# Attention beside a two-layer MLP on one core: one attention slot between any two parts of layer 1, a new order of each engine's work within a slot, and a second batch with float32 second products

## The chip, the cores and the metric

The kernel runs on one core of one Trainium2 chip. The metric is the device time of one execution in microseconds (us). A core has five engines that each take their own instructions strictly in order and wait for one another through semaphores: TensorE (PE; its weight loads are shown apart as PEld), VectorE (DVE), ScalarE (ACT), GpSimd (POOL), and SyncE (SP), which here only issues transfers. Matrix products land in PSUM, eight banks of 128 x 512 float32; everything else lives in SBUF.

## What is computed

Four batches, eight heads, 576 positions, head size 64. Attention is masked by blocks of 64, its output is the input of two dense layers with a nonlinearity between their halves; all arithmetic keeps float32 precision.

```python
scores = scale * np.matmul(q, k.transpose(0, 1, 3, 2))       # 4 x 8 heads, 576 x 576
scores = np.where(block_i >= block_j, scores, -1000000000.0)  # blocks of 64
scores = scores - np.max(scores, axis=-1, keepdims=True)
attn = np.exp(scores)
attn = attn / (np.sum(attn, axis=-1, keepdims=True) + 1e-09)
x = np.matmul(attn, v)                                        # -> 2304 tokens x 512
h = x @ w_in                                                  # layer 1: 512 -> 2048 -> 512
x = (np.maximum(h, 0.0) + alpha * np.minimum(h, 0.0)) @ w_out
h = x @ w2_in                                                 # layer 2, same sizes
out = np.where(h > 0.0, h, np.exp(np.minimum(h, 0.0)) - 1.0) @ w2_out
```

## The kernel before, in words

**Split products.** Most products are made of two-part numbers: a value is rounded to float32r ("high") and the rest is kept as a second float32r number ("low", made by `low_part`). A layer's product then takes three passes (high x high, high x low, low x high). The products of the layers are groups of 12 matmuls of 128 x 512.

**Attention.** Heads are taken in 16 pairs, four pairs to a batch. A pair is cut into five slots, and `slot(k)` handles slot `i = k % 5` of pair `k // 5`: its scores on PE (into one of two PSUM tiles, `pair0` and `pair1`, in turn), the row maxima on DVE, the exponentials on ACT, then the normalising factors on DVE and the normalising itself on POOL (`p`). The same call also transposes on PE what was exponentiated four slots earlier (`LAG = 4`) and moves the result out of PSUM into the tile `pt`.

**Second products** (attention weights times v). For the first `WHOLE` pairs `pt` is moved once, as float32, and the second products are float32, with the two heads of a pair in the two column halves of the array (`emit_pv_whole`). For the other pairs `pt` and v are split into a high and a low part (ACT and DVE for `pt`, POOL for v), and the products are float32r (`emit_pv`): head x = 0, then x = 1, each followed by an ACT copy and a DVE addition into the tile `xt`, from which POOL makes the two parts of x. Each pair has two halves: queries 0 to 255 ("half 0") and 256 to 575 ("half 1").

**Beside it.** When batch u is done, layer 1's first half of hidden units is run on it while the attention of batch u + 1 goes on (`l1_beside`): 8 "h parts" (12 matmuls, an ACT copy `h`, an ACT `neg`, a DVE `g`, an ACT and a POOL operation for the two parts of `g`), then 8 "y parts" of 12 matmuls. `att_events` gives every slot and every second product a cost, and the loop at the end of the kernel runs events until their cost has kept up with the parts done. PSUM bank 7 holds layer 1's products, banks 4 to 6 take transposes and second products in turn.

**Weights.** `load_w` fetches a 128 x 1024 block of weights and rounds it in five stages, each issued a given number of ticks after the load (`later`): ACT reads it (`wword`), DVE cuts the bits, POOL adds, ACT rounds (`w`, high), DVE subtracts (`w`, low). There are two buffers for the raw block and two for `wword`. Six blocks are loaded in the lead (before layer 1 starts), ten beside batch 1, and 48 in the rest.

**The rest.** After the attention follow steps of one h group and, two steps later, one y group: layer 1's first half on the last two units ("A"), its second half on all five ("B"), layer 2 ("C"). Units are 512, 512, 512, 512 and 256 tokens. Weights are loaded at the steps that `w_at` names.

Of the kernel before, what the change touches and what calls it, by code (L numbers as in the profile page):

```python
# [19 lines left out]
P = 128  # L20
# [21 lines left out]
def attention_moe_kernel(ctx: ExitStack, tc: tile.TileContext, qT, kT, v_a, v_b, w1, w2, alpha, out):  # L42
# [134 lines left out]
    WHOLE = 4  # L177
# [108 lines left out]
    def transposes(n, i):  # L286
# [66 lines left out]
    def emit_pv_whole(n, half):  # L353
# [11 lines left out]
        parts, tail = parts_of_x(n, half)  # L365
        for c, dst in parts:
            act.copy(dst(0), op[:, c])
            low_part("v", dst(1), op[:, c], dst(0))
        x_out(n, half, tail)

    def emit_pv(n, half):
# [3 lines left out]
        xt = ap1.tile([P, 320], F32, tag="xt", name="xt")  # L375
        op = None
        for x in range(2):
            if half or not x:
                op = bank[take("o")]
            o_ = op[:, qn * x:qn * x + qn] if half == 0 else op[:, :qn]  # L380
            for j in range(nch):
                rows = 64 if j == 4 else P
                lo, o = max(0, P * j - q0), place(half, j)
                for k in range(2):
                    pe.matmul(o_[:, lo:qn], s["vs"][:rows, 5 * x + j, :, :].rearrange("p a d -> p (a d)"),  # L385
                              s["pt", half, k][:rows, x, o + lo:o + qn],
                              start=j == 0 and k == 0, stop=j == nch - 1 and k == 1, skip_group_check=True)
            main, other = slice(64 * x, 64 * x + 64), slice(64 - 64 * x, 128 - 64 * x)
            act.copy(xt[main, :qn], o_[other, :])
            dve.tensor_tensor(out=xt[main, :qn], in0=o_[main, :], in1=xt[main, :qn], op=ALU.add)  # L390
        parts, tail = parts_of_x(n, half)
        for c, dst in parts:
            copy("p", dst(0), xt[:, c])
            low_part("p", dst(1), xt[:, c], dst(0))
        x_out(n, half, tail)
# [3 lines left out]
    COST_S, COST_T = (.33, .35, .5, .7, .8), (.22, .44, .66, .88, .5)  # L399
    LAG = 4  # L400
    NS = 5 * len(PAIRS)

    def slot(k):
# [7 lines left out]
        if i == 0 and n:  # L411
            normalise(n - 1, 2)
        if here:
            maxima(n, i)
        if move:
            move()
        if here:
            exponentials(n, i)
            if i == 0 and n + 1 < len(PAIRS):
                load_pair(n + 1)  # L420
            if i == 1:
                load_v(n)

    def att_events():
        slots = {}

        def at(k, order, cost, emit, done=None):
            here = slots.setdefault(k, [])
            here.append((order, len(here), cost, emit, done))

        for k in range(NS + LAG):
            cost = (COST_S[k % 5] if k < NS else 0) + (COST_T[(k - LAG) % 5] if k >= LAG else 0)
            at(k, 0, cost, lambda k=k: slot(k))
        for n, (b, p) in enumerate(PAIRS):
            k = 5 * n
            if n + 1 < len(PAIRS):
                at(k + 2, 3, 0, lambda n=n: split_k(n + 1))
                at(k + 3, 3, 0, lambda n=n: split_q(n + 1))
            last = b if p == NPAIR - 1 else None
            pv = emit_pv_whole if n < WHOLE else emit_pv  # L440
# [262 lines left out]
```

## Time and profile before

| | us |
|---|---|
| median of three runs | 1184.72 (1184.21 to 1184.79) |
| the profiled execution, its own time | 1185.07 |
| its span from the first to the last instruction | 1183.0 |
| PE busy | 1032.0 (87%) |
| DVE busy | 607.7 (51%) |
| ACT busy | 473.6 (40%) |
| POOL busy | 399.4 (34%) |

How to read it: busy time is an average over stages that are limited by different things. The first scores start at 5.6 us. The lead (attention alone) ends at 93.9 us, when layer 1's first group starts; the first groups of the units beside batches 1, 2 and 3 start at 93.9, 243.4 and 360.0 us; the attention is over and stage A begins at 468.7 us; B's first group starts at 548.0 and C's at 759.8 us. The profile names an instruction by its line, the engine, the tile written and the tiles read, with the shapes. An idle time is put down to the instruction that ended it.

### The profile page before, as it was taken

The page shows a single profiled execution, that of the slowest core. Times are in us where ns is not written, and L with a number is a line of the kernel's source. Part 1 is how long each engine was busy: PE and PEld are TensorE (multiplying, and loading weights), DVE is VectorE, ACT ScalarE, POOL GpSimd, SP SyncE. Part 2 cuts the span into 40 slices and gives each one's busy share as a digit, 9 for nine tenths or more (in the row PEclk, how much of TensorE's full clock was granted, in tenths as well). Part 3 has the DMA queues.
Part 4 walks back from the last instruction along what each step waited for, and adds up shares of the span by engine and source line. Part 5 has one row for each costly group of instructions (what it writes and reads, how often), then busy time and mean ns, then how long its engine had stood idle before and what let it go on. Part 6 is the DMA issues. An engine that isn't in the chain of part 4 may idle for free.

```text
span 1183.0 us, 14068 instructions
## 1 busy us (share of the span) xinstructions
PE 1032.0 (87%) x5072; PEld 839.8 (71%) x5072; DVE 607.7 (51%) x1087; ACT 473.6 (40%) x1037; POOL 399.4 (34%) x484
## 2 busy tenths in 40 slices
PE   6867657888888798987899999969899999999998
PEld 4545445666666677876788888857688888888887
DVE  5765777445544552655354564576753333333343
ACT  4655554335534551545333434444432222222222
POOL 5655656445644642544344344422200000000000
PEclk9878787988899989988899999989999999999999
DMA  3432321112121012354355444442120020010000
GB/s 98 146 102 97 105 90 51 68 51 68 51 88 48 30 40 95 115 194 139 130 168 171 160 134 169 161 179 89 54 107 1 1 107 1 1 71 1 1 37 18
DMA packets 50468, 101.57 MB, mean 86 GB/s; under 512 B 10592, under 2 KB 18784, under 8 KB 49760
## 3 DMA queue, kind: packets, MB, share of 16 engines
q1 hardware_dynamic: 50400, 100.69, 25.1%
q8 instruction: 40, 0.66, 0.2%
q14 instruction: 28, 0.23, 0.1%
HBM read 72.36 MB, written 28.31 MB: 85 GB/s over the span
## 4 chain that ended last, share of the span: by engine, by line
PE 53%; DVE 20%; ACT 13%; issue 6%; DMA 4%; POOL 4%; SPq 1%; ACTq 0%; POOLq 0%; DVEq 0%
PE bank L544 14%; PE bank L526 13%; PE bank L480 7%; PE bank L503 6%; PE bank L568 5%; DMA wraw<-w 3%; DVE wword L132 3%; PE bank L385 3%; DVE w L81 3%; DVE g L467 2%; ACT wword L125 2%; ACT wraw L126 2%; DVE wword L131 2%; PE pair L234 2%; ACT p L264 2%
## 5 line engine op out<-in xcount | busy, mean ns | idle before, releaser
L480 PE MATMUL bank<-x,w 128*128 128x512 f32 (+1 forms) x960 | 223.8, 385 | 4.3 <-DVE z L87 2.4
L544 PE MATMUL bank<-w,gs 128*128 128x512 f32 x864 | 213.9, 394 | 15.5 <-DVE z L575 9.1
L526 PE MATMUL bank<-x,w 128*128 128x512 f32 (+1 forms) x960 | 210.2, 368 | 0.0
L480 PEld LDWEIGHTS bank<-x,w 128*128 128x128 f32 x960 | 175.7, 199 | 37.3 <-DVE z L87 3.6
L544 PEld LDWEIGHTS bank<-w,gs 128*128 128x128 f32 x864 | 162.1, 190 | 52.3 <-issue 9.5
L526 PEld LDWEIGHTS bank<-x,w 128*128 128x128 f32 x960 | 169.1, 188 | 31.1
L81 POOL TENSOR_TENSOR gs<-g,gs 128x512 fp32r<-128x512 f32 (+1 forms) x80 | 96.5, 1206 | 224.5 <-ACT gs L470 212.9
L568 PE MATMUL bank<-gs,w 128*128 128x512 f32 (+1 forms) x672 | 149.8, 371 | 19.1 <-ACT z L85 8.8
L568 PEld LDWEIGHTS bank<-gs,w 128*128 128x128 f32 x672 | 118.5, 197 | 42.7 <-ACT z L85 9.4
L137 POOL TENSOR_TENSOR wword<-wword,wraw 128x512 int32<-128x512 int32 x64 | 92.7, 1449 | 93.7 <-DVE wword L132 63.1
L531 DVE TENSOR_SCALAR e<-e 128x512 f32<-128x512 f32 (+1 forms) x80 | 32.0, 400 | 179.2 <-ACT e L530 179.2
L530 ACT ACTIVATE e<-bank 128x512 f32<-128x512 f32 (+1 forms) x80 | 44.1, 551 | 161.3 <-PE bank L526 161.3
L385 PE MATMUL bank<-pt,vs 128*128 128x320 f32 (+4 forms) x336 | 58.5, 313 | 47.1 <-DVE xt L390 45.3
L467 DVE SCALAR_TENSOR_TENSOR g<-neg,beta,bank 128x512 f32<-128x512 f32 (+1 forms) x56 | 37.5, 669 | 120.4 <-ACT neg L466 118.9
L88 POOL TENSOR_SCALAR p<-p,stat 128x128 f32<-128x128 f32 (+2 forms) x144 | 80.1, 573 | 40.4 <-DVE stat L275 23.1
L385 PEld LDWEIGHTS bank<-pt,vs 128*128 128x128 f32 (+1 forms) x336 | 53.1, 203 | 53.5 <-DVE xt L390 47.0
L125 ACT ACTIVATE wword<-wraw 128x512 f32<-128x512 f32 x64 | 42.9, 670 | 111.5 <-DVE w L81 74.6
L264 ACT ACTIVATE p<-pair,stat 128x128 f32<-128x128 f32 (+3 forms) x128 | 66.4, 526 | 42.0 <-DVE stat L253 35.8
L535 ACT CAST gs<-e 128x512 fp32r<-128x512 f32 (+1 forms) x80 | 46.2, 578 | 84.9 <-DVE e L532 84.9
L132 DVE SCALAR_TENSOR_TENSOR wword<-wraw,wword 128x512 uint32<-128x512 uint32 x64 | 78.4, 1225 | 2.2
L503 PE MATMUL bank<-gs,w 128*128 128x512 f32 x288 | 77.1, 422 | 2.2 <-ACT z L85 2.2
L81 DVE TENSOR_TENSOR gs<-e,gs 128x512 fp32r<-128x512 f32 (+1 forms) x80 | 51.0, 638 | 42.5 <-ACT gs L535 42.5
(84 smaller groups left out, 1278.3 us busy)
## 6 DMA issues: line engine op xcount, KB each, us to landing
wraw<-w SPq DMA_DIRECT2D x64, 512.0 KB, 3.7
xd<-x SPq DMA_DIRECT2D x16, 512.0 KB, 3.1
x<-xd SPq DMA_DIRECT2D x16, 512.0 KB, 8.6
yd<-ys SPq DMA_DIRECT2D x16, 512.0 KB, 3.4
x<-yd SPq DMA_DIRECT2D x4, 2048.0 KB, 8.3
qraw<-qT SPq DMA_DIRECT2D x16, 288.0 KB, 2.8
kraw<-kT SPq DMA_DIRECT2D x16, 288.0 KB, 3.2
vraw<-v_a SPq DMA_DIRECT2D x16, 256.0 KB, 3.3
```

What stands on the lines that cost most here:

```text
L81: return {"v": dve, "p": pool_e}[eng].tensor_tensor(out=out, in0=x, in1=f32(high), op=ALU.subtract)
L88: return pool_e.tensor_scalar(out, x, 1.0 if scale is None else scale, 1.0, ALU.mult, ALU.mult)
L125: act.activation(out=w, in_=high.bitcast(F32), func=AF.Abs)
L132: dve.scalar_tensor_tensor(out=wi, in0=high, scalar=0xC0000000, in1=wi, op0=ALU.bitwise_and, op1=ALU.bitwise_or)
L137: pool_e.tensor_tensor(out=w, in0=w, in1=units, op=ALU.add)
L264: act.activation(out=p[:, x, :], in_=sb[:, x, :ext], func=AF.Exp, bias=stat[:, o + x:o + x + 1], accum_out=stat[:, 4 + o + x:5 + o + x])
L385: pe.matmul(o_[:, lo:qn], s["vs"][:rows, 5 * x + j, :, :].rearrange("p a d -> p (a d)"), s["pt", half, k][:rows, x, o + lo:o + qn], start= ...
L480: pe.matmul(h, w_in(0, f, wp_, kc), x[:, xp_, kc, :n], start=kc == 0 and t == 0, stop=kc == KC - 1 and t == 2)
L503: pe.matmul(acc, w_out(0, f, wp_, m * P, P), gs[f][:, gp_, :n], start=f == 0 and t == 0, stop=f == FH - 1 and t == 2)
L526: pe.matmul(h, w_in(1, f, wp_, kc), x[:, xp_, kc, :], start=kc == 0 and t == 0, stop=kc == KC - 1 and t == 2)
L544: pe.matmul(acc, gs[:, gp_, tg * P:(tg + 1) * P], w_out(1, f, wp_, 0, DM), start=f == 0 and t == 0, stop=f == NF - 1 and t == 2)
L568: pe.matmul(acc, w_out(0, f, wp_, m * P, P), gs[:, gp_, :n], start=first and t == 0, stop=last and t == 2)
```

## The change

Five things change.

1. **A slot between any two parts.** Layer 1 beside a batch is cut into 20 parts (8 h parts of 12 matmuls, and 12 y parts of 9, 9 and 6), and one attention slot follows each. The list of events with costs is gone. The lead takes 27 slots (0 to 26) where it took 26.
2. **Second products inside a slot.** They are issued to PE right behind the slot's scores and ahead of its transposes; what empties their PSUM bank is issued behind the maxima and ahead of the moves of `pt`. Half 0 comes one slot later than before. Of a split pair, both heads of half 0 are issued before either is read, and the two heads of half 1 stand in two slots.
3. **The gate is held.** DVE's `g` of an h part is issued in the slot behind it, behind that slot's maxima, and its two parts behind the slot's exponentials.
4. **`WHOLE = 8`.** Batch 1 (pairs 4 to 7) has float32 second products as batch 0 has. Which of ACT and DVE moves which part of a float32 `pt` changes as well.
5. **Weights.** Eight blocks are loaded in the lead, one every third slot, and eight beside batch 1, one for each of its first eight parts. In stage A the last eight blocks of layer 1's second half are spread thinner (steps 8, 10, 12, 14 and 16 to 19); layer 2's first half is loaded at steps 20 to 35, one a step, where it was every other step from 19 to 49; its second half starts two steps before C, where it was four.

```diff
-    WHOLE = 4
+    WHOLE = 8
...
-                    copy("av"[(m + i) % 2], dst(pt[0]), src)
+                    copy("a" if m == 0 and i else "v", dst(pt[0]), src)
...
+    def products(k):
+        todo = []
+        n, i = divmod(k - LAG - 4, 5)
+        if i == 0 and 0 <= n < len(PAIRS):
+            todo += [lambda: pv_whole(n, 0)] if n < WHOLE else [lambda: pv(n, 0, 0), lambda: pv(n, 0, 1)]
+        m, i = divmod(k - LAG - 6, 5)
+        if 0 <= m < len(PAIRS) and i < 2:
+            if m >= WHOLE:
+                todo.append(lambda: pv(m, 1, i))
+            elif i == 0:
+                todo.append(lambda: pv_whole(m, 1))
+        return todo
...
         if here:
             scores(n, i)
+        outs = [p() for p in products(k)]
         move = transposes(*divmod(k - LAG, 5)) if 0 <= k - LAG < NS else None
...
         if here:
             maxima(n, i)
+        after = [h() for h in held]
+        held.clear()
+        for o in outs:
+            o()
         if move:
             move()
         if here:
             exponentials(n, i)
+        for a in after:
+            a()
...
-        pv = emit_pv_whole if n < WHOLE else emit_pv
-            at(k + LAG + 3, 2, .75, lambda n=n, pv=pv: pv(n, 0))
-            at(k + LAG + 6, 2, 2.3, lambda n=n, pv=pv: pv(n, 1), last)
...
-                if f % 4 == 3:
+                if f in (2, 5, 7):
...
-        W_AT = (8, 12, 16, 20, 24, 28)
+        lead = X_DONE[0] + 2
+        for k in range(lead):
+            if k % 3 == 0 and k and len(todo_w) > FH:
+                load_w(*todo_w.pop(0))
+            slot(k)
...
         for u in range(B - 1):
+            parts = l1_beside(u)
+            for j in range(20):
+                if todo_w:
+                    load_w(*todo_w.pop(0))
+                next(parts)
+                if k < LAST:
+                    slot(k)
+                    k += 1
...
+        spread = [*range(8), *range(8, 16, 2), *range(16, 20)]
-            w_at[i] = (0, FH + half[0], half[1])
-            w_at[first_of["B", 0] + lag + 1 + 2 * i] = (1, *half)
-            w_at[first_of["B", NU - 1] + lag + 2 + i] = (1, FH + half[0], half[1])
+            w_at[spread[i]] = (0, FH + half[0], half[1])
+            w_at[spread[-1] + 1 + i] = (1, *half)
+            w_at[first_of["C", 0] - 2 + i] = (1, FH + half[0], half[1])
```

PE's instructions around half 0 of a split pair, before: transposes (`ident`), the eight second products (`vs`) into bank 102, then layer 1's y part (`gs`) into bank 104.

```order
L310 MATMUL bank_103<-ident,p 128x128 x4
L310 MATMUL bank_101<-ident,p 128x128 x4
L385 MATMUL bank_102<-pt_1691,vs 128x256
L385 MATMUL bank_102<-pt_1692,vs 128x256
L385 MATMUL bank_102<-pt_1691,vs 128x128
L385 MATMUL bank_102<-pt_1692,vs 128x128
L385 MATMUL bank_102<-pt_1691,vs 128x256
L385 MATMUL bank_102<-pt_1692,vs 128x256
L385 MATMUL bank_102<-pt_1691,vs 128x128
L385 MATMUL bank_102<-pt_1692,vs 128x128
L503 MATMUL bank_104<-gs,w 128x512 x12
```

The same place in the changed kernel: an h part of layer 1 (`x`), the next slot's scores (`pair`), the eight second products, then the transposes.

```order
L499 MATMUL bank_104<-x_1061,w 128x512 x12
L234 MATMUL pair_100<-kh,qh 128x512 x2
L234 MATMUL pair_100<-kl,qh 128x512 x2
L234 MATMUL pair_100<-kh,ql 128x512 x2
L386 MATMUL bank_103<-pt_2068,vs 128x256
L386 MATMUL bank_103<-pt_2069,vs 128x256
L386 MATMUL bank_103<-pt_2068,vs 128x128
L386 MATMUL bank_103<-pt_2069,vs 128x128
L386 MATMUL bank_103<-pt_2068,vs 128x256
L386 MATMUL bank_103<-pt_2069,vs 128x256
L386 MATMUL bank_103<-pt_2068,vs 128x128
L386 MATMUL bank_103<-pt_2069,vs 128x128
```

The eight rows themselves are the same; what stands between the first four and the last four on the other engines has moved, as DVE's order shows. Before, DVE took `g` as soon as its h part was issued, and the two additions into `xt` behind it, ahead of the next slot's maximum (`stat<-pair`):

```order
L81 TENSOR_TENSOR pt_2323<-bank_101,pt_2322 128x4x128
L81 TENSOR_TENSOR pt_2323<-bank_102,pt_2322 128x4x128
L467 SCALAR_TENSOR_TENSOR g<-neg,beta,h 128x512
L390 TENSOR_TENSOR xt<-bank_103,xt 64x256 x2
L252 MEMSET pair_100 64x2x64
L253 TENSOR_REDUCE stat<-pair_100 128x2
```

Now the maximum comes first, then the held `g`, then the additions into `xt`, then the moves of `pt`:

```order
L252 MEMSET pair_99 64x2x64
L253 TENSOR_REDUCE stat<-pair_99 128x2
L482 SCALAR_TENSOR_TENSOR g<-neg,beta,h 128x512
L396 TENSOR_TENSOR xt<-bank_103,xt 64x256 x2
L81 TENSOR_TENSOR pt_2907<-bank_101,pt_2906 128x4x2x64
L81 TENSOR_TENSOR pt_2907<-bank_102,pt_2906 64x2x64
L211 SCALAR_TENSOR_TENSOR ql<-qraw,qh 128x512
```

So `g` and the additions moved behind the maximum of the slot that follows the h part.

ACT's instructions in a slot of the lead that has half 1 of a float32 pair, before: the move of `pt`, the exponentials (`p,stat<-pair`) of two slots with two weight operations between them, and then the two casts of x that empty the second products' bank.

```order
L85 COPY pt_521<-bank_101 128x2x128
L268 ACTIVATE p,stat<-pair_99,stat 128x576
L125 ACTIVATE wword<-wraw 128x512
L126 ACTIVATE wraw<-wraw 128x512
L264 ACTIVATE p,stat<-pair_100,stat 128x128 x2
L367 CAST x_312<-bank_104 128x256
L367 CAST xtail<-bank_104 128x64
```

Now the casts come first, then the move, then the slot's own exponentials:

```order
L268 ACTIVATE p,stat<-pair_99,stat 128x576
L370 CAST x_343<-bank_104 128x256
L370 CAST xtail<-bank_104 128x64
L85 COPY pt_536<-bank_102 128x2x256
L264 ACTIVATE p,stat<-pair_100,stat 128x128 x2
```

The exponentials moved behind the second products, the casts that read them, and the move.

## Rows read from the trace of the kernel before

**Rows 1.** Busy time by stage; the stretch and its length come first.

```profile
core 0: us, PE busy (x) PEld busy (x) DVE busy (x) ACT busy (x) POOL busy (x), PEclk, DMA share, GB/s
0.00:93.90 93.90, 64.83 (x375) 41.80 (x375) 61.49 (x151) 50.45 (x144) 53.67 (x91) 0.84 0.35 113
93.90:197.70 103.80, 62.80 (x308) 49.36 (x308) 75.86 (x123) 55.66 (x128) 61.40 (x70) 0.79 0.26 88
197.70:243.40 45.70, 40.53 (x219) 32.67 (x217) 20.76 (x49) 16.80 (x48) 21.48 (x37) 0.96 0.23 76
243.40:360.00 116.60, 97.30 (x524) 78.21 (x524) 58.65 (x130) 55.74 (x146) 63.08 (x96) 0.91 0.18 60
360.00:468.70 108.70, 92.37 (x483) 74.59 (x483) 49.00 (x105) 49.08 (x122) 51.74 (x77) 0.92 0.14 46
468.70:571.00 102.30, 87.23 (x433) 74.99 (x434) 59.31 (x87) 46.85 (x90) 46.74 (x35) 0.90 0.46 154
731.00:866.00 135.00, 116.88 (x579) 96.53 (x578) 90.84 (x139) 57.71 (x110) 38.83 (x31) 0.96 0.36 127
```

**Rows 2.** Who waited for whom, 93.9 to 468.7 us: total, times, longest.

```profile
PE bank L385 <- DVE xt L390: 45.3, 12, 7.9
...
DVE g L467 <- ACT neg L466: 45.7, 19, 4.7
...
PE bank L310 <- DVE pt L81: 12.3, 7, 3.6
```

**Rows 3.** Timeline, 253 to 258 us: start, length, instruction, idle before and its end.

```profile
253.48 0.57 PE L385 MATMUL bank<-pt,vs 128*128 128x256 f32 x4
...
255.15 0.75 DVE L467 SCALAR_TENSOR_TENSOR g<-neg,beta,h 128x512 f32<-128x512 f32 x1 [1.30 <-ACT neg L466]
...
256.58 0.37 ACT L389 COPY xt<-bank 64x256 f32<-64x256 f32 x1
...
256.98 0.42 DVE L390 TENSOR_TENSOR xt<-bank,xt 64x256 f32<-64x256 f32 x1 [1.08 <-ACT xt L389]
...
257.45 1.11 PE L385 MATMUL bank<-pt,vs 128*128 128x256 f32 x4 [3.40 <-DVE xt L390]
```

**Rows 4.** Timeline of PE in stage B, two groups that follow each other.

```profile
576.35 2.88 PE L480 MATMUL bank<-x,w 128*128 128x512 f32 x12
579.07 2.88 PE L568 MATMUL bank<-gs,w 128*128 128x512 f32 x12
```

**Rows 5.** Busy time of `wword` instructions alone: DVE, ACT, POOL, then clock and DMA.

```profile
0.00:93.90 93.90, 14.21 (x24) 7.72 (x12) 7.70 (x6) 0.84 0.35 113
93.90:197.70 103.80, 38.36 (x41) 12.86 (x20) 14.17 (x10) 0.79 0.26 88
```

**Rows 6.** Timeline of PE, half 0 of a float32 pair in the lead.

```profile
24.17 0.92 PE L362 MATMUL bank<-pt,vraw 128*64 128x256 f32 x8
```

**Rows 7.** Busy time by stretch, columns as rows 1: half 1 whole, then half 1 split.

```profile
30.87:34.90 4.03, 4.03 (x21) 1.85 (x20) 3.46 (x8) 1.76 (x7) 4.03 (x6) 0.58 0.66 240
266.88:270.10 3.22, 3.22 (x24) 2.94 (x21) 2.00 (x6) 2.37 (x7) 1.70 (x3) 1.00 0.18 69
```

**Rows 8.** Timeline of ACT in stage C, one weight block a step.

```profile
811.70 0.67 ACT L125 ACTIVATE wword<-wraw 128x512 f32<-128x512 f32 x1 [3.26 <-DVE w L81]
812.27 0.65 ACT L126 ACTIVATE wraw<-wraw 128x512 int32<-128x512 uint32 x1
...
818.50 0.67 ACT L125 ACTIVATE wword<-wraw 128x512 f32<-128x512 f32 x1 [3.26 <-DVE w L81]
```

**Rows 9.** Timeline, waits in stages A to C: a transfer and two PSUM banks.

```profile
533.93 0.66 ACT L125 ACTIVATE wword<-wraw 128x512 f32<-128x512 f32 x1 [8.69 <-DMA wraw<-w]
...
565.94 5.10 PE L568 MATMUL bank<-gs,w 128*128 128x512 f32 x12 [5.84 <-ACT z L85]
...
780.81 5.16 PE L544 MATMUL bank<-w,gs 128*128 128x512 f32 x12 [9.06 <-DVE z L575]
```

**Rows 10.** Who waited for whom in the lead, 0 to 93.9 us.

```profile
PE pair L234 <- ACT p L264: 8.7, 4, 3.7
```

More of the change, by code (lines that the diff above doesn't have):

```diff
@@ L364, in emit_pv_whole, with out, pv @@
                           start=j == 0, stop=j == nch - 1, skip_group_check=True)
[L365 to L371, printed above, removed]
+        def out():
+            parts, tail = parts_of_x(n, half)
+            for c, dst in parts:
+                act.copy(dst(0), op[:, c])
+                low_part("v", dst(1), op[:, c], dst(0))
+            x_out(n, half, tail)
+        return out
+    def pv(n, half, x):
         s = st[n]
@@ L374, in emit_pv @@
         nch = 2 if half == 0 else 5
[L375 to L387, printed above, removed]
-            main, other = slice(64 * x, 64 * x + 64), slice(64 - 64 * x, 128 - 64 * x)
-            act.copy(xt[main, :qn], o_[other, :])
-            dve.tensor_tensor(out=xt[main, :qn], in0=o_[main, :], in1=xt[main, :qn], op=ALU.add)
@@ L391, in emit_pv @@
[L391 to L399, printed above, removed]
+        if half or not x:
+            s["op"] = bank[take("o")]
+        op = s["op"][:, :qn] if half else s["op"][:, qn * x:qn * x + qn]
+        for j in range(nch):
+            rows = 64 if j == 4 else P
+            lo, o = max(0, P * j - q0), place(half, j)
+            for k in range(2):
+                pe.matmul(op[:, lo:], s["vs"][:rows, 5 * x + j, :, :].rearrange("p a d -> p (a d)"),
+                          s["pt", half, k][:rows, x, o + lo:o + qn],
+                          start=j == 0 and k == 0, stop=j == nch - 1 and k == 1, skip_group_check=True)
@@ new lines, in out @@
+        def out():
+            main, other = slice(64 * x, 64 * x + 64), slice(64 - 64 * x, 128 - 64 * x)
+            if x == 0:
+                s["xt"] = ap1.tile([P, 320], F32, tag="xt", name="xt")
+            xt = s["xt"]
+            act.copy(xt[main, :qn], op[other, :])
+            dve.tensor_tensor(out=xt[main, :qn], in0=op[main, :], in1=xt[main, :qn], op=ALU.add)
+            if x == 1:
+                parts, tail = parts_of_x(n, half)
+                for c, dst in parts:
+                    copy("p", dst(0), xt[:, c])
+                    low_part("p", dst(1), xt[:, c], dst(0))
+                x_out(n, half, tail)
@@ L403, in slot @@
+    held = []
     def slot(k):
@@ L418, in slot @@
             exponentials(n, i)
[L419 to L439, printed above, removed]
-            pv = emit_pv_whole if n < WHOLE else emit_pv
-            at(k + LAG + 3, 2, .75, lambda n=n, pv=pv: pv(n, 0))
-            at(k + LAG + 6, 2, 2.3, lambda n=n, pv=pv: pv(n, 1), last)
-            if n >= WHOLE:
-                at(k + LAG + 1, 3, 0, lambda n=n: split_v(n))
-        return [e[2:] for k in sorted(slots) for e in sorted(slots[k], key=lambda e: e[:2])]
-    def run(event):
-        cost, emit, _ = event
-        emit()
-        if cost:
-            end_tick()
+        for a in after:
+            a()
+        if i == 0 and n + 1 < len(PAIRS):
+            load_pair(n + 1)
+        if i == 1 and here:
+            load_v(n)
+        if i == 2 and n + 1 < len(PAIRS):
+            split_k(n + 1)
+        if i == 3 and n + 1 < len(PAIRS):
+            split_q(n + 1)
+        m, j = divmod(k - LAG - 2, 5)
+        if j == 0 and WHOLE <= m < len(PAIRS):
+            split_v(m)
+        end_tick()
+    X_DONE = [5 * (NPAIR * b + NPAIR - 1) + LAG + 6 + (NPAIR * (b + 1) > WHOLE) for b in range(B)]
     def load_x1(u):
@@ L466, in l1_gate, with gate @@
         act.activation(out=neg, in_=h, func=AF.Relu, scale=-1.0)
-        dve.scalar_tensor_tensor(out=g, in0=neg, scalar=beta[:, f:f + 1], in1=h, op0=ALU.mult, op1=ALU.add)
+        def gate():
+            dve.scalar_tensor_tensor(out=g, in0=neg, scalar=beta[:, f:f + 1], in1=h, op0=ALU.mult, op1=ALU.add)
+            return parts
         def parts():
@@ L471, in parts @@
             low_part("p", t[:, 1, :], g, t[:, 0, :])
-        later(1, parts)
+        if beside:
+            held.append(gate)
+        else:
+            later(1, gate())
         return t
@@ L605, in attention_moe_kernel @@
         ring("h", 7)
[L608 removed]
+        k = lead
         for u in range(B - 1):
[L610 to L626 removed]
+            parts = l1_beside(u)
+            for j in range(20):
+                if todo_w:
+                    load_w(*todo_w.pop(0))
+                next(parts)
+                if k < LAST:
+                    assert k <= X_DONE[u + 1] or j >= 18
+                    slot(k)
                     k += 1
[L628 to L629 removed]
+        assert k == LAST and not held
         att.close()
```

37 lines of the change are left out of this document (6 added, 31 removed).

## The prediction

> **What bounds the kernel now.** I read the busy time by stage first [rows 1]. PE is busy for most of the span, but not evenly: in the first stretch beside batch 1 (93.9 to 197.7 us) for 62.80 of 103.80 us, beside batches 2 and 3 for 97.30 of 116.60 and 92.37 of 108.70 us. Its granted clock tells the same: 0.79 in the first of these, 0.91 and 0.92 in the others, so part of the time it ran at 1.2 and not at 2.4 GHz. No other engine is full there either; DVE's 75.86 of 103.80 us is the most. So the three units beside batches 1 to 3, 374.8 us in all, are bound by waits between engines, with DVE near its limit while weights are being rounded.
>
> The list of who waited for whom names the largest wait of PE in these units [rows 2]: 45.3 us in 12 waits, a second product waiting for DVE's addition into `xt`. That is 3.8 us in each of the 12 split pairs. A timeline shows how one comes about [rows 3]. PE does the first head of half 0 and may not write the second head's products into the same bank until DVE has read the first. But ACT's copy stands behind the h part's copy, `neg` and two parts, and DVE's addition stands behind `g`: 3.40 us of idle PE for a copy of 0.37 and an addition of 0.42 us. DVE itself lost 45.7 us waiting for `neg`, with `g` at the head of its queue and the next maximum behind it.
>
> Behind the attention PE is nearly full: two groups of 12 matmuls follow each other every 2.72 us at full clock [rows 4]. The waits that are left stand in stage A, at A's end and where C begins [rows 9].
>
> **The change, part by part.**
>
> *PE's floor beside a batch.* Busy time times granted clock gives the work in full-clock time [rows 1]: 62.80 x 0.79 + 40.53 x 0.96 = 88.5 us for the unit beside batch 1, 97.30 x 0.91 = 88.5 and 92.37 x 0.92 = 85.0 for the others. Layer 1 has 16 groups of 2.72 us in each [rows 4], 43.5 us; the rest, 45 us, is attention, 2.25 us a slot. So a step with an h part needs 2.72 + 2.25 = 4.97 us of PE and one with a y part (8 matmuls on average, 1.81 us) 4.06 us. 8 x 4.97 + 12 x 4.06 = 88.5.
>
> *The wait for `xt`* goes away: in the new order both heads of half 0 are issued before either is read, and the heads of half 1 stand in two slots. What comes late next is the emptying of three banks in turn, which each slot's transposes and second products need. It has the next part, 2.72 or 1.81 us, and its scores as cover; ACT's and DVE's work on a split move is about one copy and one subtraction a bank, so I count it as covered, and as up to 1 us a slot if ACT runs late.
>
> *The held gate* takes `neg` off DVE's head. POOL waits longer for the two parts, which are wanted only in the y parts.
>
> *Units beside batches 2 and 3*, no weights to round there: the floor of 88.5 and 85.0 us plus short waits. I take 6% for these, a third of what the second stretch beside batch 1 has over its clocked work (45.70 against 38.9 us [rows 1], the `xt` waits among it): 94 us and 91 us (this one has seven slots without scores, but starts with its last pair's x only just issued, some 3 us that nothing covers; stage A starts so too). The bounds are the floors, and the present 116.6 and 108.7 less 15 each for the `xt` waits of four pairs: 101.6 and 93.7.
>
> *The unit beside batch 1* rounds eight blocks in its first steps. Rounding costs DVE 14.21 / 6 = 2.37 us a block in the lead and 38.36 / 10 = 3.84 beside layer 1 [rows 5]. I take 3.84, the same neighbourhood. DVE's attention work with float32 second products is the lead's, (61.49 - 14.21) / 26 = 1.82 us a slot [rows 1, 5]; with `g`, 0.75 [rows 3], a step has 6.41 us. ACT's two readings of the next block (0.67 + 0.65) wait for DVE's last operation on an earlier one, as they do in stage C, where that ring sets a step of 6.80 us [rows 8]. The ring is 6.41 + 1.32 = 7.73; I take 8.0. Eight such steps, 64 us, one of 4.97 ahead, one of 6 behind, and ten of 4.26: 117.6, say 117, where it is now 103.80 + 45.70 = 149.5. The GPSIMD Engine Reference of the Trainium skill (1. Specifications) says that GpSimd's SBUF interfaces are shared with VectorE and contend with some of its instructions. The trace agrees as far as 2.37 against 3.84 us goes; by the lower price, were POOL out of the way, the sum would be 12 us smaller.
>
> *Float32 second products in batch 1* take ACT, DVE and POOL work off that unit (the 1.82 holds it). On PE a whole pair costs 0.92 + 4.03 us, the latter at a clock of 0.58 [rows 6, 7], and a split pair 2 x 0.57 + 3.22 at full clock [rows 3, 7]: 4.95 against 4.36, or 0.92 + 2.34 = 3.26 at full clock. Over four pairs that is between 2.4 us more and 4.4 us less; I count nothing. The page FP8 and Floating Point Precision of the Trainium skill (TensorE Precision Notes) says that true float32 takes four passes through the array. By that, against the split form's two products and with nothing running side by side, a pair would cost twice 4.36, and the sum would be 17 us larger. The trace disagrees: 4.95 us at a low clock.
>
> *The lead* had 3.4 us a slot ((93.9 - 5.6) / 26, with the first scores at 5.6 us) and gets one more slot and two more blocks. Half of their 4.7 us of DVE work shows, since DVE is busy 65% of the lead [rows 1, 5]; the earlier start, at slot 3, gives some back. 93.9 + 3.4 + 1 = 98 us; bounds 92 and 106.
>
> *Stages A to C* take 1183.0 - 468.7 = 714.3 us. From 468.7 to 571.0 us PE's clocked work is 87.23 x 0.90 = 78.5 us: 24 us are lost, some of them at A's end, where banks are emptied late because ACT is busy with weights (5.84 us [rows 9]), and in steps of 256 columns, which PE does faster than a block is rounded. The thinner loads should give back 10 us of it; the wait for a weight transfer [rows 9], behind the transfers of x, stays. Layer 2's loads at every step of 2 x 2.72 us in B nearly fit: 3 us lost at unit boundaries. From 731 to 866 us 135.0 - 116.88 x 0.96 = 23 us are lost. C's loads start two steps later: the wait of 9.06 us where C begins shrinks, and the steps of 6.80 us go on two steps longer: 1 us gained. The uncovered start costs 3 us. 710 us; bounds 696 and 722.
>
> **Sum:** 98 + 117 + 94 + 91 + 710 = 1110 us of span; the profiled execution has 2.1 us around its span of 1183.0, and is 0.3 us above the median. So 1112 us.
>
> **The rivals.**
>
> 1. *Only the `xt` waits go.* The waits of steps with weights stay as they are: ten blocks now take 103.80 us, eight would take 83, and the unit 83 + 11 + 43 = 137; the others 101.6 and 93.7, the rest 714, the lead 100: 1146 us of span, 1148 us. For it: the queues stay in order, and POOL's part of the ring (rounding, the gate's low part, k and q) stands at each slot's end. Against it: in rows 2 the largest waits are the two that the new order takes away.
> 2. *Slower: exponentials behind the second products.* ACT now takes a slot's exponentials only when that slot's second products, casts, transposes and moves are through; scores two slots on need the PSUM tile they read. If PE and ACT took turns with nothing side by side, a step would be PE's 88.5 / 20 = 4.43 us and ACT's 55.74 / 20 = 2.79 [rows 1], 7.2 us. I price it at three quarters of ACT's share, 6.5 us: 60 steps are 391 us, with the lead of 98 and the rest at 714 a span of 1203, 1205 us. It decides from 6.2 us a step, where the three units take the 375 us that they take now. For it: the lead has 8.7 us of just this wait [rows 10]. Against it: with two tiles in turn the exponentials have two steps of PE's time, and layer 1's part in each, before PE asks for them.
> 3. *More is gained:* PE stays at full clock beside the attention, the units reach the floors, the ring runs at 6.8 us, the lead and A to C their lower bounds: 92 + 107 + 88 + 85 + 696 = 1068, or 1070 us.
>
> **How the numbers follow.** Forecast (1065 to 1140 us around 1112): 0.66. Rival 1 (1140 to 1180): 0.20. Rival 3 below 1065: 0.05. Rival 2: 0.06. No change within 0.2%, 2.4 us, about what a measurement of this kernel can tell from none: 0.03. The range 1065 to 1160 takes the forecast, and most of rival 1; what is outside it is 0.05 + 0.06 + 0.03 and the upper third of rival 1. Faster 0.91, same 0.03, slower 0.06.
>
> **What would show it.** No PE wait for `xt` at the second products, against 45.3 us; DVE's wait for `neg` gone; first groups of the units at about 98, 215, 309 and, for stage A, 400 us; a clock of 0.95 or more beside batches 2 and 3; weight steps of about 8 us beside batch 1, with ACT waiting for DVE's `w`. It is wrong if PE waits at scores for `p`, at transposes for the moves of `pt`, or at second products for POOL's `vs`, more than 1 us a slot.

## The result, and the profile after

The changed kernel takes 1103.68 us (median of four runs, 1103.53 to 1105.81), the kernel before 1184.76: a ratio of 0.9315, 95% interval 0.9295 to 0.9335. The prediction said 1112 (1065 to 1160) and faster. The profiled execution took 1103.71 us, its span is 1101.9.

| stage | before | predicted | after |
|---|---|---|---|
| lead | 93.9 | 98 | 88.6 |
| beside batch 1 | 149.5 | 117 | 111.4 |
| beside batch 2 | 116.6 | 94 | 90.4 |
| beside batch 3 | 108.7 | 91 | 85.0 |
| A | 79.3 | | 74.2 |
| B | 211.8 | | 221.4 |
| C | 423.2 | | 430.9 |
| A to C together | 714.3 | 710 | 726.5 |

The stages are cut at the first groups of matmuls as before. Here is the busy time by stage, to be read against [rows 1]; the unit beside batch 1 is cut once more where its first y part starts.

```profile
core 0: us, PE busy (x) PEld busy (x) DVE busy (x) ACT busy (x) POOL busy (x), PEclk, DMA share, GB/s
0.00:88.60 88.60, 62.36 (x387) 39.80 (x387) 64.37 (x155) 50.49 (x144) 54.37 (x92) 0.92 0.38 125
88.60:150.50 61.90, 42.34 (x223) 30.38 (x220) 48.26 (x77) 38.66 (x89) 35.28 (x38) 0.89 0.35 114
150.50:200.00 49.50, 48.56 (x303) 35.20 (x304) 30.66 (x72) 24.37 (x69) 26.60 (x38) 0.97 0.26 88
200.00:290.40 90.40, 88.53 (x527) 70.99 (x526) 59.51 (x132) 55.17 (x147) 61.85 (x90) 1.00 0.26 83
290.40:375.40 85.00, 81.90 (x473) 66.71 (x471) 49.56 (x104) 48.59 (x122) 54.52 (x77) 1.00 0.17 59
375.40:449.60 74.20, 67.65 (x360) 58.61 (x361) 42.18 (x60) 32.83 (x64) 34.00 (x29) 0.95 0.44 150
449.60:671.00 221.40, 204.92 (x963) 168.52 (x961) 112.77 (x153) 91.62 (x167) 92.10 (x70) 0.97 0.47 157
671.00:1101.90 430.90, 406.32 (x1850) 335.56 (x1848) 189.61 (x319) 121.96 (x220) 26.46 (x19) 0.98 0.14 48
```

Beside batches 2 and 3 PE is busy for 88.53 of 90.40 and 81.90 of 85.00 us, at full clock throughout: these units stand close to the floor, with 1.9 and 3.1 us of idle PE. DVE, ACT and POOL do as much there as before, so nothing was saved; the waits went, and the low clock with them. The gain up to stage A is 468.7 - 375.4 = 93.3 us; A to C give 12.2 back, which the prediction did not see.

Who waited for whom on PE, 88.6 to 375.4 us, to be read against [rows 2]; these are all of PE's waits there:

```profile
PE bank L499 <- ACT h L514: 9.7, 7, 2.4
PE bank L522 <- ACT h L514: 9.3, 3, 7.9
PE bank L302 <- DVE x L81: 2.9, 2, 1.6
PE bank L310 <- DVE xtail L81: 1.5, 1, 1.5
PE bank L522 <- DVE w L81: 0.9, 1, 0.9
PE bank L386 <- POOL vs L81: 0.2, 1, 0.2
```

The wait for `xt` (45.3 us) is gone, and DVE waits for `neg` 1.3 us instead of 45.7. What is left is 19 us for ACT's copy `h` out of bank 7, 15.2 of them beside batch 1. The longest, 7.9 us at the first y part, comes for the most part from the ring of weight buffers: ACT waits 4.85 us for DVE's last operation on an older block and only then comes to the copy.

```profile
148.78 0.66 ACT L125 ACTIVATE wword<-wraw 128x512 f32<-128x512 f32 x1 [4.85 <-DVE w L81]
...
149.90 0.57 ACT L514 COPY h<-bank 128x512 f32<-128x512 f32 x1
```

The timeline of a split pair's half 0 beside batch 2, to be read against [rows 3], shows how it goes now:

```profile
233.78 0.50 PE L234 MATMUL pair<-kh,qh 64*128 64x512 f32 x2
...
234.67 1.14 PE L386 MATMUL bank<-pt,vs 128*128 128x256 f32 x8
...
235.65 0.62 PE L316 MATMUL bank<-ident,p 128*128 128x128 f32 x4
...
236.14 2.98 PE L499 MATMUL bank<-x,w 128*128 128x512 f32 x12
236.19 0.74 DVE L482 SCALAR_TENSOR_TENSOR g<-neg,beta,h 128x512 f32<-128x512 f32 x1
236.85 0.41 DVE L396 TENSOR_TENSOR xt<-bank,xt 64x256 f32<-64x256 f32 x1
```

All eight second products run together in 1.14 us, the transposes and the next h part follow, and `g` and the additions fall under that h part.

Behind the attention it is the other way round. The timeline of PE at the end of a unit in B, and where C's rounding ends:

```profile
565.69 1.62 PE L587 MATMUL bank<-gs,w 128*128 128x512 f32 x3 [7.09 <-DVE z L594]
...
763.69 4.63 PE L545 MATMUL bank<-x,w 128*128 128x512 f32 x10 [3.75 <-DVE w L81]
...
777.26 4.64 PE L545 MATMUL bank<-x,w 128*128 128x512 f32 x10 [3.76 <-DVE w L81]
```

In B the additions `z` that empty PE's banks stand on DVE behind roundings that are in arrears; in C, PE waits for the weights themselves. The groups right behind each wait run at a granted clock of 0.50, the lower level: 10 matmuls take 4.63 us, where 12 take 2.88 at full clock [rows 4].

### The profile page after: what moved, and what is told of

The parts are those of the page before. It is cut to its first block, busy times and chain, and to the rows that moved or that the text cites. A ratio compares the mean times of both kernels' runs of the same rounds, so it can differ in the third digit from the quotient of the medians.

```text
span 1101.9 us, 14026 instructions
## 1 busy us (share of the span) xinstructions
PE 1002.6 (91%) x5072; PEld 805.8 (73%) x5072; DVE 596.9 (54%) x1067; ACT 463.7 (42%) x1017; POOL 385.2 (35%) x452
## 4 chain that ended last, share of the span: by engine, by line
PE 54%; DVE 18%; ACT 9%; issue 5%; POOL 3%; DMA 3%; SPq 0%; ACTq 0%; POOLq 0%; DVEq 0%
PE bank L563 15%; PE bank L545 15%; PE bank L499 7%; PE bank L522 5%; PE bank L587 4%; DVE wword L132 4%; DVE w L81 4%; DMA wraw<-w 3%; PE bank L386 3%; ACT wword L125 2%; DVE g L482 2%; PE pair L234 2%; ACT wraw L126 2%; DVE wword L131 2%; PE bank L310 2%
## 5 line engine op out<-in xcount | busy, mean ns | idle before, releaser
L545 PEld LDWEIGHTS bank<-x,w 128*128 128x128 f32 x960 | 171.5, 191 | 43.7 <-DVE w L81 8.4
L499 PEld LDWEIGHTS bank<-x,w 128*128 128x128 f32 x960 | 169.7, 192 | 42.8 <-ACT h L514 11.8
L587 PEld LDWEIGHTS bank<-gs,w 128*128 128x128 f32 x672 | 116.9, 195 | 49.5 <-issue 13.2
L137 POOL TENSOR_TENSOR wword<-wword,wraw 128x512 int32<-128x512 int32 x64 | 96.4, 1506 | 95.9 <-DVE wword L132 67.2
L88 POOL TENSOR_SCALAR p<-p,stat 128x128 f32<-128x128 f32 (+2 forms) x144 | 85.6, 612 | 61.7 <-DVE stat L275 43.2
L132 DVE SCALAR_TENSOR_TENSOR wword<-wraw,wword 128x512 uint32<-128x512 uint32 x64 | 75.3, 1176 | 2.2
L81 DVE TENSOR_TENSOR w<-wword,w 128x512 fp32r<-128x512 f32 x64 | 66.5, 1039 | 7.2 <-ACT w L145 7.2
L522 PEld LDWEIGHTS bank<-gs,w 128*128 128x128 f32 x288 | 52.6, 193 | 20.9 <-ACT h L514 10.0
```

Source lines behind the costliest of these rows:

```text
L81: return {"v": dve, "p": pool_e}[eng].tensor_tensor(out=out, in0=x, in1=f32(high), op=ALU.subtract)
L88: return pool_e.tensor_scalar(out, x, 1.0 if scale is None else scale, 1.0, ALU.mult, ALU.mult)
L132: dve.scalar_tensor_tensor(out=wi, in0=high, scalar=0xC0000000, in1=wi, op0=ALU.bitwise_and, op1=ALU.bitwise_or)
L137: pool_e.tensor_tensor(out=w, in0=w, in1=units, op=ALU.add)
L499: pe.matmul(h, w_in(0, f, wp_, kc), x[:, xp_, kc, :n], start=kc == 0 and t == 0, stop=kc == KC - 1 and t == 2)
L522: pe.matmul(acc, w_out(0, f, wp_, m * P, P), gs[f][:, gp_, :n], start=f == 0 and t == 0, stop=f == FH - 1 and t == 2)
```

## Experiments

All ratios are to the kernel before on the same chip. The runs stand on several chips, so small costs are better read from the ratios than from the times. A to C differ by up to 4 us between runs with the same steps there, so stage lengths count beside the totals.

**The weights behind the attention**

*e1, C's loads four steps ahead.*

```diff
-            w_at[first_of["C", 0] - 2 + i] = (1, FH + half[0], half[1])
+            w_at[first_of["C", 0] - 4 + i] = (1, FH + half[0], half[1])
```

> One number is undone: layer 2's second half is loaded from four steps before C on, as in the kernel before, instead of two. Theory: in the changed kernel PE waits in C for weight blocks that are not rounded yet (four waits of 1.20, 3.75, 1.64 and 3.76 us between 759 and 778 us, and a clock of 0.5 around them); with the loads two steps earlier these go, and a longer wait where C begins (2.93 us now, 9.06 us in the kernel before) comes back: C takes 423 us, as in the kernel before, instead of 430.9, and the run about 1096 us. Rival (the prediction's own reckoning): loading two steps later gained 1 us, so undoing it gives 1105 us.

1099.37 us, ratio 0.9262 (0.9229 to 0.9296), whose interval just touches the change's. C took 423.1 us, B 225.2. PE no longer waits for weights in C; the wait where C begins is back as it was in [rows 9], in PE's timeline:

```profile
696.54 5.06 PE L563 MATMUL bank<-w,gs 128*128 128x512 f32 x12 [9.06 <-DVE z L594]
```

So the theory holds for C (423); 3.8 us of it are paid in B, into whose last unit the loads now reach.

*e2, B's loads at every second step.*

```diff
-            w_at[spread[-1] + 1 + i] = (1, *half)
+            w_at[spread[-1] + 1 + 2 * i] = (1, *half)
```

> One number is undone: layer 2's first half is loaded at every second step of B, from step 20 on, instead of at every step. Theory: loads at every step ask for a rounding every 5.44 us where the chain of roundings needs about 5.7, DVE falls behind, and at two ends of units in B the additions that empty PE's banks come 5.30 and 7.09 us late, each followed by a stretch at half clock; undone, B takes about 211.8 us, as in the kernel before, instead of 221.4: the run about 1094 us. Rival (the prediction's reckoning): 3 us are lost there, so about 1101 us. If neither, 1104 us: the waits belong to something else.

1099.86 us, ratio 0.9262 (0.9227 to 0.9297); B took 216.7 us. Half of the expected 9.6 us: the waits of 5.30 and 7.09 us went, but the short ones for the additions `zl` at the units' ends grew from 3.3 us in 6 waits to 9.2 in 8. That the ring needs 5.7 us is seen where ACT reads two blocks in the changed kernel's B, each reading waiting for DVE's last operation on an older block:

```profile
542.81 0.67 ACT L125 ACTIVATE wword<-wraw 128x512 f32<-128x512 f32 x1 [2.55 <-DVE w L81]
548.52 0.67 ACT L125 ACTIVATE wword<-wraw 128x512 f32<-128x512 f32 x1 [2.56 <-DVE w L81]
```

*e3, all three as before.* Beside the two edits above:

```diff
-        spread = [*range(8), *range(8, 16, 2), *range(16, 20)]
+        spread = [*range(16), 18]
```

> All three changes of the weight schedule behind the attention are undone together (stage A loads at every step, except that its last block stands at step 18; B at every second step; C from four steps ahead). Theory: stages A to C lost by the change, 726.5 us against 714.3 in the kernel before; undone they take about 714 and the run 1091 to 1092 us. Rival (the prediction): the thinner loads gain 10 us in A and cost 2 elsewhere, so undoing all three would make the run about 1108 to 1112 us.

1094.47 us, ratio 0.9221 (0.9182 to 0.926). The list's last number, 18, only puts B's first load at step 19; A's sixteen blocks stand at steps 0 to 15, as in the kernel before, and not with one at step 18. A 81.1, B 213.1, C 423.3 us: the new weight schedule costs 9 us in all. Its thinner loads in A gain 6.9 us, its parts in B and C lose 8.3 and 7.6. The prediction's reckoning for A to C had the wrong sign.

*e4, a third buffer behind the attention.*

```diff
-    wt, ready = {}, set()
+    wt, ready, words = {}, set(), [0]
...
-            w = wraw_p.tile([P, DM], F32, tag="wword", name="wword")
+            words[0] += 1
+            p_, n_ = (late_pools[0], 1) if late_pools and words[0] % 3 == 0 else (wraw_p, 2)
+            w = p_.tile([P, DM], F32, tag="wword", name="wword", bufs=n_)
```

> Behind the attention a third buffer for the block being rounded (wword) is added, and nothing else. Theory: what sets the step with a weight block is the ring of two buffers (ACT may not read block i+2 before DVE's last operation on block i, and everything behind ACT's reading waits with it); with a third buffer steps of 6.80 us in C fall to about 5.5, the four waits of C for unrounded blocks go, and B's late ends shrink from 5.30 and 7.09 us to 2 or less: the run about 1075 us. Rival: the operations of DVE and POOL themselves set the step (DVE is busy for 64.2 of the 90.2 us in which C's blocks are rounded), and the buffer is no matter: 1101 to 1104 us.

1075.31 us, ratio 0.9065 (0.903 to 0.91). ACT's timeline in C, first the changed kernel, then this one:

```profile
729.74 0.67 ACT L125 ACTIVATE wword<-wraw 128x512 f32<-128x512 f32 x1 [3.26 <-DVE w L81]
...
736.55 0.67 ACT L125 ACTIVATE wword<-wraw 128x512 f32<-128x512 f32 x1 [3.26 <-DVE w L81]
```

```profile
718.42 0.68 ACT L127 ACTIVATE wword<-wraw 128x512 f32<-128x512 f32 x1 [1.30 <-DMA wraw<-w]
...
723.31 0.68 ACT L127 ACTIVATE wword<-wraw 128x512 f32<-128x512 f32 x1 [1.29 <-DMA wraw<-w]
```

ACT now waits for the transfer and no longer for DVE's last operation, and these two blocks are 4.89 us apart where they were 6.81 (5.5 on average over C's blocks); PE's steps go at 5.44 us. C is 23.7 us shorter, B 3.3 and A 2.1. So in C it was the ring of two buffers, not the engines' work, that set the step; DVE does more in the same time (77.55 us in the first 90.2 of C, where it did 64.18).

*g3, e4 and e2 together.*

> The third buffer of e4 and the loads at every second step of B of e2 together. Theory: the two take away different waits in B (with the third buffer, additions that come 0.81 and 3.64 us late and a stretch at half clock behind each still stand at the ends of the first two units): 4 us less than e4, about 1071 us. Rival: what is left in B belongs to the transfers of weights and not to their rate, or the loads that now reach further into B cost as much at the later ends of units: 1074 to 1078 us.

1074.42 us, ratio 0.9062 (0.9041 to 0.9083): no different from e4. B took 217.0 us against 218.1: the rival. With the third buffer the rate of loads hardly matters.

**The order beside layer 1**

*f1, the second head's products after the first head's reads.*

```diff
+            if x == 0 and half == 0:
+                pv(n, 0, 1)()
...
-            todo += [lambda: pv_whole(n, 0)] if n < WHOLE else [lambda: pv(n, 0, 0), lambda: pv(n, 0, 1)]
+            todo += [lambda: pv_whole(n, 0)] if n < WHOLE else [lambda: pv(n, 0, 0)]
```

> Of a split pair's half 0, the second head's products are issued only after the first head's copy and addition into xt, which stand where they stand now (behind the maxima and the gate); the products themselves are unchanged. Theory: the wait that the prediction took away (3.8 us in each split pair) comes back, shortened by the transposes that PE now has ahead of it, about 1 us: 8 split pairs by 2.8 us are 22 us, so about 1126 us, with PE waiting at the second products for xt and a lower clock beside batches 2 and 3. Rival: with one slot between any two parts the time goes elsewhere anyway (PE would wait as long at the next scores): 1104 to 1108 us.

1113.84 us, ratio 0.9384 (0.9347 to 0.9421). The units beside batches 2 and 3 took 95.2 and 89.6 us. PE's waits there:

```profile
PE bank L386 <- DVE xt L396: 9.2, 8, 1.9
```

The wait is back in each of the 8 pairs, but at 1.15 us instead of 3.8, and the clock is 0.98 in both units: the theory is right in kind, its size is not.

*f2, the gate not held.*

```diff
-            gs[f] = l1_gate(f, copied, n, True)
+            gs[f] = l1_gate(f, copied, n)
```

> The gate of the units beside batches 1 to 3 is issued right behind its h part again, ahead of the next slot, as in the kernel before; all else is as in the changed kernel. Theory (the prediction's): DVE then stands at g until ACT has made neg, 2.4 us in each of 24 h parts as before (45.7 us in 19 waits), and the next maximum with everything behind it comes that much later. Where DVE is nearly full (eight steps beside batch 1) that is 19 us; beside batches 2 and 3, where DVE is idle a third of the time, less than half of it, some 15 us: about 1125 to 1135 us. Rival: DVE's wait lies beside PE's h part and its scores, and costs nothing: 1102 to 1106 us.

1112.26 us, ratio 0.9366 (0.9337 to 0.9395). DVE waits for `neg` again, 22.6 us in 12 waits beside batches 2 and 3, but these units took 91.3 and 86.2 us, 2 us more together; the unit beside batch 1 took 114.1, 2.7 more.

```profile
DVE g L482 <- ACT neg L479: 22.6, 12, 2.8
```

Alone, the wait lies beside PE's work; neither theory nor rival has the size, the rival is nearer.

*g1, both undone, and the second products at the slot's end again.*

```diff
-        outs = [p() for p in products(k)]
...
-        for o in outs:
-            o()
...
+        for p in products(k):
+            p()()
...
-            gs[f] = l1_gate(f, copied, n, True)
+            gs[f] = l1_gate(f, copied, n)
```

> The order within a slot is that of the kernel before: second products stand at the slot's end, each head's products followed at once by its copy and addition, and the gate is not held. One slot between any two parts, WHOLE = 8 and the weights stay as in the changed kernel. Undone one at a time, reading between the heads cost 10 us and the gate not held 9. Theory A: the two hold each other up (the copy behind neg and the h copy on ACT, the addition behind g on DVE), so that the order is what made the units beside batches 2 and 3 26 and 24 us shorter; with both undone they go back to some 110 and 103 us, and the run takes about 1150 us. Theory B: the two costs add up and the rest of the gain came from the even spacing of the slots: 1120 to 1126 us, with those units near 96 and 91 us.

1163.32 us, ratio 0.9816 (0.98 to 0.9832): 60 us more than the change, where the two parts alone came to 10 and 9 (by the ratios 59, against 8 and 6; in the three units 54 us, against 9.5 and 4.8). Busy time by unit, beside batches 1 to 3, then PE's waits beside batches 2 and 3, then the timeline of one pair:

```profile
93.60:213.00 119.40, 95.88 (x523) 68.63 (x524) 74.18 (x150) 63.51 (x155) 58.36 (x75) 0.91 0.29 94
213.00:324.60 111.60, 96.92 (x527) 76.99 (x525) 58.65 (x130) 55.62 (x145) 61.01 (x90) 0.91 0.21 69
324.60:434.60 110.00, 92.77 (x472) 74.25 (x471) 49.41 (x104) 49.68 (x123) 53.27 (x78) 0.89 0.13 45
```

```profile
PE bank L386 <- DVE xt L396: 28.3, 8, 5.3
```

```profile
253.80 0.66 PE L386 MATMUL bank<-pt,vs 128*128 128x256 f32 x4
254.02 0.63 ACT L478 ACTIVATE neg<-h 128x512 f32<-128x512 f32 x1
254.75 1.08 DVE L481 SCALAR_TENSOR_TENSOR g<-neg,beta,h 128x512 f32<-128x512 f32 x1 [1.37 <-ACT neg L478]
...
256.05 1.23 DVE L253 TENSOR_REDUCE stat<-pair 128x2 f32<-128x1024 f32 x1
...
257.37 0.69 ACT L264 ACTIVATE p<-pair,stat 128x512 f32<-128x512 f32 x1 [0.25 <-DVE stat L253]
...
258.84 0.37 ACT L395 COPY xt<-bank 64x256 f32<-64x256 f32 x1
259.24 0.42 DVE L396 TENSOR_TENSOR xt<-bank,xt 64x256 f32<-64x256 f32 x1 [1.18 <-ACT xt L395]
```

The first head is done at 254.46 us, and its copy starts at 258.84, behind `neg` and the exponentials on ACT, and these behind `g` and the maximum on DVE: two queues that wait for one another, as in [rows 3]. The units are within 5 us of the kernel before and the clock is low again: theory A. Nearly the whole gain beside batches 2 and 3 is the order within a slot; even spacing with the old order gives next to nothing (3.7 us). The reverse, the new order without even spacing, was not run. The lead is 93.6 us, so 5 us of the lead's gain are of this order too. Beside batch 1 it is otherwise: with the old order that unit takes 119.4 us, so 30.1 of its 38.1 us come with the old order too.

**Batch 1 and the lead**

*f3, WHOLE = 4 again* (that one number).

> WHOLE is 4 again: batch 1 has split second products as in the kernel before; all else is as in the changed kernel. Theory: in the eight steps with a weight block, DVE's time sets the step, and the moves of a split pt and the xt additions cost it more than the moves of a whole one (59.5 us in 20 slots beside batch 2 less 6 for g, 2.7 a slot, against the 1.82 counted): 0.9 us by 8 steps, 7 us, so about 1111 us, all of it between the first h part and the first y part beside batch 1. Rival 1: PE's time decides, and float32 products at half clock cost more than split ones: up to 10 us less, 1094 to 1100 us. Rival 2: four passes for a float32 product, without running side by side, would make the split form 17 us faster: 1087 us.

1117.8 us, ratio 0.9407 (0.9376 to 0.9439). Busy time of the unit beside batch 1, up to its first y part and behind it:

```profile
90.50:159.50 69.00, 46.80 (x223) 34.94 (x221) 54.64 (x86) 41.87 (x95) 44.20 (x48) 0.85 0.31 98
159.50:212.40 52.90, 51.41 (x304) 41.23 (x305) 38.28 (x83) 28.81 (x80) 35.44 (x52) 0.97 0.27 91
```

7.1 us more in the first stretch, as the theory has it, and 3.4 more behind it. So float32 second products are worth 10.5 us in this unit; what two blocks fewer and the even spacing give there was not separated. DVE, ACT and POOL do 14.0, 7.7 and 17.8 us more in this unit, and PE's busy time by its clock is 46.80 x 0.85 + 51.41 x 0.97 = 89.6 us, against 84.8 in the changed kernel. Float32 second products are the faster form here, against both rivals, on PE too. The page FP8 and Floating Point Precision of the Trainium skill (TensorE Precision Notes) has four passes for float32; by that, and with nothing running side by side, the prediction reckoned the split form 17 us faster, and this run shows the opposite. It does not speak against the four passes. Half 1 of a float32 pair, at full clock in the changed kernel:

```profile
154.81 2.42 PE L363 MATMUL bank<-pt,vraw 128*64 128x320 f32 x20
```

Half 1 has 3 x 320 + 192 + 64 = 1216 columns a head. As an estimate by the pace of [rows 4] (12 x 512 columns in 2.72 us), four passes of both heads would take 4.3 us one after the other and 2.15 us side by side: the 2.42 us fit the two column halves working at the same time.

*f4, the moves of a float32 `pt` alternate as before.*

```diff
-                    copy("a" if m == 0 and i else "v", dst(pt[0]), src)
+                    copy("av"[(m + i) % 2], dst(pt[0]), src)
```

> ACT and DVE move the parts of a float32 pt in the old alternation again (ACT first in even slots); all else is as in the changed kernel. Theory: the lead went from 3.4 to 3.07 us a slot because second products stand ahead of the transposes, and not because of who copies: 1102 to 1107 us, with the first h part within 2 us of 88.6. Rival: the assignment of the moves is what made the lead and the first unit shorter: the first h part near 97, and the run 1112 us or more.

1106.55 us, ratio 0.9317 (0.929 to 0.9343), the first h part at 89.0 us: no matter, as expected.

*g2, DVE's last operation on a block one tick earlier.*

```diff
-        later(6, last)
+        later(6 if late_pools else 5, last)
```

> In the lead and beside batch 1 DVE's last operation on a weight block is issued one tick earlier (right behind ACT's rounding, ahead of the next slot), so that ACT's reading of the block after the next is no longer issued just behind it; all else is as in the changed kernel. Theory (the prediction's ring): this reading waits for that operation in each of the eight steps beside batch 1; the first to the eighth step fall from 7 to 8 us to below 7, the unit by 5 to 8 us, the run to 1096 to 1099 us. Rival 1: the operations of DVE and POOL themselves fill the step: within 2 us of 1104. Rival 2: DVE now stands at the operation until ACT and POOL are through, ahead of the slot's maximum, and the unit gets 5 us longer: 1109 us.

1120.53 us, ratio 0.9451 (0.9433 to 0.9469): rival 2, and dearer than it said. The unit took 121.3 us, the lead 92.1. DVE now stands at its last operation for ACT's rounding (23.4 us in 7 waits before the first y part), with the slot's maximum behind it.

```profile
DVE w L81 <- ACT w L145: 23.4, 7, 5.9
```

*h1, the third buffer from the start.* Beside `bufs=3` for `wword`, `z` has one buffer during the attention.

```diff
-            w = wraw_p.tile([P, DM], F32, tag="wword", name="wword")
+            w = wraw_p.tile([P, DM], F32, tag="wword", name="wword", bufs=3)
...
+        zcount[0] += 1
+        if zcount[0] % 2 and late_pools:
+            return late_pools[0].tile([P, 512], F32, tag="z", name="z", bufs=1)
-        return gp.tile([P, 512], F32, tag="z", name="z", bufs=2)
+        return gp.tile([P, 512], F32, tag="z", name="z", bufs=1)
```

> The third buffer of e4 from the start, in the lead and beside batch 1 too; the room comes from layer 1's output tile z, which has one buffer during the attention instead of two (the second one is made behind it). Theory (the prediction's ring): ACT's reading no longer waits for DVE's last operation on a block beside batch 1, where it waits 5.6 us in all now, 4.85 us of it once; the stretch from the first h part to the first y part, 61.9 us in the changed kernel and in e4, falls to 53 to 58 us and the run to 1067 to 1072 us. Rival, for which g2 speaks: beside batch 1 it is not the buffer but the number of operations on DVE, POOL and ACT between two h parts that sets the step, and ACT only waits elsewhere: that stretch stays within 1.5 us of 61.9, and the run at 1074 to 1077 us.

1073.67 us, ratio 0.9056 (0.9032 to 0.9079), not to be told from e4: the total is outside the theory's 1067 to 1072 us. Busy time of the unit beside batch 1:

```profile
87.10:143.20 56.10, 43.06 (x222) 30.75 (x220) 43.43 (x70) 38.46 (x88) 33.87 (x35) 0.91 0.36 119
143.20:196.70 53.50, 50.13 (x304) 36.06 (x305) 32.97 (x78) 24.27 (x69) 29.38 (x42) 0.94 0.27 88
```

The first stretch fell from 61.9 to 56.1 us, as the theory says; the second grew from 49.5 to 53.5. Four of DVE's last operations on a block now come behind the first y part, where it was three; PE waits 3.3 us there once at the transposes, and its clock is 0.94 where it was 0.97. So the ring costs the stretch with the weights 5.8 us, of which 4.0 are given back behind it. What sets the 56.1 us that are left was not separated; DVE is busy for 43.4 of them.

## Why the prediction was right, and where it was not

- **The `xt` wait and the held gate.** Right: both waits vanished. What the prediction did not say is how they hang together: it took them for separate waits, and f1, f2 and g1 show that they are not. Which of the three edits in g1 (the second products behind the transposes, the reading between the heads, the gate) make the chain was not separated further.
- **The units beside batches 2 and 3.** The floor from busy time times clock was right for the first (88.5, measured 88.53 at full clock) and 3 us too high for the second (85.0, measured 81.90). Of the 6% of short waits on top, 1.9 and 3.1 us were there. These two terms were 3.6 and 6.0 us too large. The clock of 0.95 or more came as 1.00.
- **The unit beside batch 1.** The eight steps with a weight block took 64.5 us (the second h part starts at 93.1 us, the second y part at 157.6) where 64 were forecast, but only on average: the steps are 5.4 to 13.4 us long. The eleven steps behind them took 42.4 us where 48.6 were forecast, and that is the error. ACT's wait for `w` is 5.9 us, 4.9 of it at once, and not one in every step. So the reason given for the 8 us, a ring that sets every step, was wrong here: with a third buffer (h1) the eight steps still take 58.7 us.
- **Float32 second products** at nothing on PE: f3 bears out that they take work off the other engines (10.5 us in this unit), and PE's 4.8 us of clocked work less are just past the lower bound of the prediction (4.4). Its reading that the trace disagrees with four passes for float32 holds only for passes one after the other (the rows at f3).
- **The lead**, 9.4 us too long, and at 88.6 us outside its bounds (92 to 106). The term of 3.4 + 1 us for a slot and two blocks failed: with the old order (g1) 27 slots and eight blocks took 93.6 us, no more than 26 slots and six blocks had. The new order then took 5.0 us off, which I had not counted at all.
- **Stages A to C: the step that failed**, 16.5 us too short, outside its bounds (696 to 722) and with the wrong sign. Its terms: the thinner loads of A gained 6.9 us (e3), not 10. "Nearly fit" in B, 3 us, was 8 to 10. A block was asked for every 5.44 us and read every 5.71 (the rows at e2), so that DVE's arrears grow up to a unit's end. That is about half of the loss: the slower rate (e2) takes 4.7 us away, the third buffer (e4) 3.3, both (g3) 4.4. The rest is open; e3, which wins back 8.3, also starts B's loads one step earlier. "1 us gained" in C was 7 to 8 lost: I counted the steps of 6.80 us as going on longer, but not that the last blocks are wanted at fixed steps, which PE then waits for. The uncovered start of A, put at 3 us, is a wait of 1.0 us.
- The errors by stage, -9.4, -5.6, -3.6, -6.0 and +16.5 us, cancel in the sum but for 8.1. That the total came within 0.8% is in part luck: two of its five terms were outside their own bounds, on opposite sides. Rival 1 and rival 2 did not show: beside the batches PE does not wait at scores for `p` at all (in the lead it does, 8.3 us, where it was 10.8), and 0.2 us in all for `vs`.

## What to carry to other kernels

When two engines hand work to each other through in-order queues, cost their waits together: here two edits undone singly cost 8 and 6 us by the ratios, and 59 together with the slot's old order. Where an engine waits for the last operation on an older buffer and no engine is full, count buffers before spreading loads: one more buffer of 2 KB a partition was worth 28 us behind the attention, where the old schedule of the loads gave back 9. A load that starts later must be followed to the step that uses it, not only to where its rate hurts.

## What was not expected

The granted clock recovered whole: beside batches 2 and 3 it is 1.00 over 175.4 us, with PE busy for 170.43 of them, while in g1 PE's waits of 28.3 us in 8 go with a clock of 0.91 and 0.89. Beside batch 2, g1's 96.92 us of busy PE at 0.91 are 88.2 us of work, against 88.53 at full clock; so of its 21.2 us more, 8.4 are clock and 12.8 idle time.
